# A fused linear-attention and bilinear-FFN kernel: dummy products to the column, g_norm out of the first place, a split load, wide weight loads and idle PSUM banks for block 1

## The chip, the cores and the metric

The kernel runs on one core of one Trainium2 chip. The metric is the device time in microseconds (us). A profile of one execution gives the span, which is some 1.7 to 2.0 us shorter than the time of the same execution; spans are compared with spans here and times with times. The granted clock is the share of TensorE's full clock that the profile records as given to it; 1.0 is full speed.

TensorE is the matmul engine, DVE the vector engine, ACT the scalar engine. POOL issues loads on a software queue; SP and ACT issue on hardware queues.

## The reference, cut to what matters

```python
# q, k, v: (8, 8, 576, 64)   w_a, w_b: (512, 1536)   w_out: (1536, 512)   fp32 in and out
kv  = np.einsum('bhsd,bhse->bhde', k, v)
out = np.einsum('bhsd,bhde->bhse', q, kv)
out = out / np.sqrt(np.mean(out * out, axis=-1, keepdims=True) + 1e-06) * g_norm
x   = out.transpose(0, 2, 1, 3).reshape(4608, 512)
return ((x @ w_a) * (x @ w_b)) @ w_out
```

## The kernel before

The kernel plans its own order. Each piece of work is a node with an engine, an estimated length, a priority and dependences with estimated latencies. A list scheduler then fixes the order of instructions on every engine. The real waits are semaphores, so a wrong estimate never gives a wrong result; it gives an order in which an engine stands still. PSUM banks, SBUF tiles and stores are rings that a node "takes" and "frees".

```python
    def order(self):            # cut
        ...
        t = max(self.ready(n), f)
        key = (f if t < f + 0.06 else t, n.prio)    # startable now: lowest prio; else earliest start
        if eng not in best or key < best[eng][0]:
            best[eng] = (key, t, n, way)
```

Batch 0 must be transposed, multiplied and normed before the FFN can start. TensorE has gaps in this stretch, and the kernel fills them with products of zeros whose result nobody reads.

```python
    def dummies(n):
        ps = banks[4]
        for _ in range(n):
            nc.tensor.matmul(ps[:], lhsT=zt[:, 0:128], rhs=zt, start=True, stop=True)
    ...
    dummies(10)
    nc.tensor.transpose(banks[5][:, 0:1], g_row, one)
    nc.vector.tensor_copy(g_col, banks[5][:, 0:1])
    ... # the plan is made here
    order, t = plan.order(), 5.7
    for n in order:
        if n.eng == "PE" and n.start < 22.0:
            dummies(int((n.start - t - 0.05) / 0.216))
            t = n.end
        n.emit()
```

Block 0 (512 tokens) uses plain products. Blocks 1 to 8 use a scheme of seven products per 2x2 block product, in six columns j. Per column there are products p1 to p7 into bank rings X, Y and Z, copies by ACT (ev), additions by DVE (comb), and at the end one multiplication of the a-half by the b-half on DVE. The last column's multiplication of block 8 is the last operand that the sums of the final output unit need.

```python
            X = Buf(RQ if bi == nb and j % 3 == 2 else RX)
            Y, Z = Buf(RY), Buf(RY)
            ... # cut
            p1 = pe(0.0, X, w_at(0, fs), lambda: b11, True, xdeps(lo, t0, t0 + n), [X])
            e1 = ev(0.0, u1, X, p1)
            ... # cut: p2, p6, p5, p7, p4, p3 with their copies and additions
            m = plan.add("DVE", fast_us(4 * n), pr + 0.6, mul, outs + [tk], (), [bb])
```

The loads of batches 2 to 7 (k and v directly, q through a transposing DMA) are planned with guessed latencies.

```python
        issue_us, q_us, ld["kv_us"] = (16.0, 5.5, 13.0) if dep is None else (9.0, 1.5, 11.5)
```

## Time and profile before

| What | Before | Where it is read |
|---|---|---|
| time, first three executions | 300.69 us (300.38 to 301.75) | times |
| span of the profiled execution | 298.7 us | first line of the page |
| TensorE busy | 290.9 us, 97% | part 1 of the page |
| block 0's first product | 16.27 us | timeline of TensorE |
| time that TensorE loses from 16 us to its last matmul | 3.58 us | start-to-start distances, below |
| last matmul's start to the end of the span | 4.0 us | timeline of TensorE |

Two of the first lines of the page of the kernel before; part 1 gives busy time, share of the span and number of instructions per engine.

```profile
span 298.7 us, 6687 instructions
PE 290.9 (97%) x2624; PEld 237.7 (80%) x2624; DVE 234.1 (78%) x433; ACT 192.5 (64%) x403; POOL 78.7 (26%) x97
```

TensorE binds the span as a whole. How much can still be won is not said by "97%", because the ends of matmuls are modelled. The view of waits of TensorE from 16 us on shows who held it; the columns are the waiting line, what released it, us in total, how often, and the longest.

```profile
PE bk L346 <- DMA qT<-scr: 1.0, 1, 1.0
PE bk L334 <- DMA abt<-in_q_dram: 0.2, 1, 0.2
PE bk L742 <- DVE T L711: 0.2, 1, 0.2
PE bk L846 <- DMA wo_t<-in_moe_w_out_dram: 0.2, 1, 0.2
```

The reader sees four waits: batch 3's transposed q, batch 1's q, block 1's operand T, and w_out. I also took the distance from one matmul's start to the next in the trace, less what the shape needs back to back (columns/2400 + 0.0025 us, which the 512-column products at 0.216 us and the 256-column ones at 0.109 us obey in this trace). It counts what the waits view drops below its threshold:

```
start   lost us   waits for
16.15   0.18      batch 0, squares by ACT
20.91   0.41      batch 1's q
44.67   0.14      block 1
45.48   0.37      block 1 (T)
47.95   0.26      block 1
65.68   0.34      w_out
80.89   1.15      batch 3's q^T
from 16 us to the last matmul: 3.58 in all
```

The lines shown are the losses of 0.14 us and more. Some 1.1 us of the sum are changes between 512-column products and groups of small ones, which take 0.09 to 0.10 us each.

The start of the kernel before: the timeline of TensorE and then of DVE. The columns are start, us, engine, line, operation, output<-input, shape and count; in brackets stand the idle time before it and who ended it.

```profile
6.21 0.19 PE L398 MATMUL bk<-one,g_row 1*128 1x1 f32 x1 [0.56 <-DMA g_row<-in_g_norm_dram]
7.11 0.56 PE L334 MATMUL bk<-ident,so 96*64 96x96 bf16 x12 [0.39 <-DVE so L494]
...
6.43 0.16 DVE L399 COPY g_col<-bk 128x1 f32<-128x1 f32 x1 [2.94 <-PE bk L398]
6.51 0.55 DVE L494 CAST so<-so 96x768 bf16<-96x768 f32 x1
```

A load of g_norm (two parts of 256 bytes) holds everything here. The transpose of g_norm stands first on TensorE and waits until 6.21; DVE copies it at 6.43; only then does DVE cast q, which had landed at 5.33, and only at 7.11 do the real transposes start.

The end of the kernel before, as the chain of waits has it from 285 us on (start, us, what):

```profile
284.93 0.22 PE bk L742 x2
285.15 9.84 PE bk L911 x90
294.99 0.03 issue
295.01 0.42 DVE o_sb L949
```

After block 8's last products (L742) stand 90 products of the final output unit (L911) without a gap, then one addition and a store. The last rows of TensorE's timeline show which products these are:

```profile
291.10 1.47 PE L911 MATMUL bk<-so,as 128*128 128x256 f16 x12
292.41 1.47 PE L911 MATMUL bk<-wo_t,as 128*128 128x256 f16 x12
293.72 1.25 PE L911 MATMUL bk<-so,abt 128*128 128x256 f16 x10
```

### The profile page before, as it was taken

The numbers are of one execution on the slowest core, as the hardware profiler recorded it, in microseconds if no ns is written. First come the engines' busy times: TensorE is split into PE (matmuls) and PEld (weight loads), VectorE is DVE, ScalarE is ACT, GpSimd is POOL, SyncE is SP. The second block draws the span as 40 slices with busy tenths as digits, with TensorE's granted clock in tenths as the row PEclk, the third lists the DMA queues.
The fourth block names the chain that finished last, engine by engine and source line by source line (L and its number), as shares of the span: only waits on it lengthen the run. The fifth ranks groups of instructions, "written<-read, shape, count | busy, mean of one in ns | idle before, by whom it ended". The sixth has DMA issues, their size and how long they took to land.

```text
span 298.7 us, 6687 instructions
## 1 busy us (share of the span) xinstructions
PE 290.9 (97%) x2624; PEld 237.7 (80%) x2624; DVE 234.1 (78%) x433; ACT 192.5 (64%) x403; POOL 78.7 (26%) x97
## 2 busy tenths in 40 slices
PE   7999999999899999999999999999999999999995
PEld 2545558855688898889888998889888888888884
DVE  4354979795878979698869986999599957897862
ACT  3757666866478667875688548954797556664521
POOL 8955830940191470190470000000000000000000
PEclk9999999999999999999999999999999999999999
DMA  8999999799999699699999400030004000300053
GB/s 178 191 200 199 195 160 157 98 167 167 235 101 164 76 201 189 56 103 165 208 142 161 143 2 0 2 143 1 2 0 143 1 2 10 133 1 2 2 170 112
DMA packets 99235, 32.72 MB, mean 110 GB/s; under 512 B 76676, under 2 KB 95108, under 8 KB 99204
## 3 DMA queue, kind: packets, MB, share of 16 engines
q0 software_dynamic: 78608, 18.44, 65.9%
q1 hardware_dynamic: 20096, 13.31, 20.4%
q10 hardware_dynamic: 500, 0.56, 0.6%
q8 instruction: 20, 0.33, 0.4%
q14 instruction: 11, 0.09, 0.1%
HBM read 37.75 MB, written 12.98 MB: 170 GB/s over the span
## 4 chain that ended last, share of the span: by engine, by line
PE 72%; DMA 21%; POOL 5%; issue 1%; DVE 0%; SPq 0%; POOLq 0%
PE bk L742 42%; PE bk L911 25%; DMA scr<-in_q_dram 8%; DMA qT<-scr 7%; DMA wb_t<-in_moe_w_b_dram 4%; DMA wa_t<-in_moe_w_a_dram 2%; PE bk L346 2%; PE bk L360 2%; PE bk L533 1%; POOL as L238 1%; POOL scr L566 1%; POOL so L238 1%; POOL wo_t L609 1%; POOL wa_t L295 1%; POOL wb_t L296 0%
## 5 line engine op out<-in xcount | busy, mean ns | idle before, releaser
L761 DVE TENSOR_TENSOR c<-bk,u 128x512 f16<-128x512 f32 x144 | 97.0, 687 | 27.2 <-ACT u L415 14.0
L415 ACT COPY u<-bk 128x512 f32<-128x512 f32 x144 | 82.3, 591 | 41.1 <-PE bk L742 38.5
L742 PE MATMUL bk<-xp,wa_t 128*128 128x256 f16 x288 | 55.0, 273 | 0.1
L742 PE MATMUL bk<-xp,wb_t 128*128 128x256 f16 x288 | 55.0, 273 | 0.0
L742 PEld LDWEIGHTS <-wa_t 128*128 128x128 f16 x384 | 37.4, 98 | 6.3 <-issue 0.3
L911 PEld LDWEIGHTS <-abt 128*128 128x128 f16 x384 | 37.5, 98 | 4.7
L369 DVE SCALAR_TENSOR_TENSOR xp<-bk,g_col,rs 128x288 f16<-128x288 f32 x64 | 32.6, 513 | 10.9 <-ACT rs L364 10.8
L742 PEld LDWEIGHTS <-wb_t 128*128 128x128 f16 x384 | 37.5, 98 | 4.4
L415 ACT CAST c<-bk 128x512 f16<-128x512 f32 x48 | 28.2, 590 | 17.6 <-PE bk L742 16.9
L911 PE MATMUL bk<-wo_t,abt 128*128 128x256 f16 x288 | 37.1, 273 | 0.0
L742 PE MATMUL bk<-T,sa 128*128 128x256 f16 x192 | 36.7, 273 | 0.2 <-DVE T L711 0.2
L742 PE MATMUL bk<-T,sb 128*128 128x256 f16 x192 | 36.7, 273 | 0.0
L364 ACT ACTIVATE rs<-bk,eps_t 128x288 f32<-128x288 f32 x64 | 32.2, 508 | 5.9 <-PE bk L360 5.4
L796 DVE TENSOR_TENSOR abt<-c 128x1024 f16<-128x1024 f16 x48 | 32.9, 688 | 1.8
L742 PEld LDWEIGHTS <-sa 128*128 128x128 f16 x288 | 28.0, 98 | 4.5 <-DVE T L711 0.5
L911 PEld LDWEIGHTS <-as 128*128 128x128 f16 x288 | 28.1, 98 | 3.5
L742 PEld LDWEIGHTS <-sb 128*128 128x128 f16 x288 | 28.1, 98 | 3.3
L356 ACT ACTIVATE sq<-bk 128x288 bf16<-128x288 f32 x64 | 25.2, 414 | 1.9 <-PE bk L346 1.7
L911 PE MATMUL bk<-so,as 128*128 128x256 f16 x192 | 25.7, 273 | 0.0
L943 ACT COPY o_sb<-bk 128x512 f32<-128x512 f32 x31 | 18.2, 587 | 11.1 <-PE bk L911 10.3
L572 POOL DMA_DIRECT2D k_t<-in_k_dram x24 | 21.2, 898 | 1.1 <-DMA wb_t<-in_moe_w_b_dram 0.5
L566 POOL DMA_DIRECT2D scr<-in_q_dram x12 | 19.6, 1635 | 1.9 <-issue 1.4
(100 smaller groups left out, 393.6 us busy)
## 6 DMA issues: line engine op xcount, KB each, us to landing
out_dram<-o_sb SPq DMA_DIRECT2D x20, 256.0 KB, 2.3
scr<-in_q_dram POOLq DMA_DIRECT2D x12, 288.0 KB, 8.0
k_t<-in_k_dram POOLq DMA_DIRECT2D x24, 128.0 KB, 8.2
v_t<-in_v_dram POOLq DMA_DIRECT2D x6, 512.0 KB, 10.1
out_dram<-o_sb SPq DMA_DIRECT2D x18, 128.0 KB, 2.3
wo_t<-in_moe_w_out_dram POOLq DMA_DIRECT2D x2, 768.0 KB, 9.4
wa_t<-in_moe_w_a_dram POOLq DMA_DIRECT2D x5, 256.0 KB, 10.8
wb_t<-in_moe_w_b_dram POOLq DMA_DIRECT2D x5, 256.0 KB, 10.8
```

The costliest lines, as they stand in the source:

```text
L238: nc.gpsimd.dma_start(out=t[n][:, hs, :, :], in_=src[b, hs].rearrange("h (sp c) d -> sp h c d", c=EC),)
L356: nc.scalar.activation(sq, self.x_ps[p, h][:, 0:HF], AF.Square)
L364: nc.scalar.activation(rs, self.s_ps[p, h][:, 0:HF], AF.Abs_reciprocal_sqrt, bias=eps_t)
L369: nc.vector.scalar_tensor_tensor(out=xcols(p, self.b * S + h * HF, HF), in0=self.x_ps[p, h][:, 0:HF], scalar=g_col, in1=self.rs[p, h], op0 ...
L415: ("ACT", act_us(n), lambda: nc.scalar.copy(*args())),
L566: nc.gpsimd.dma_start(out=scr[:, :, hl, :].rearrange("p s d -> s p d"), in_=qv[hl])
L572: nc.gpsimd.dma_start(out=kt[:, c], in_=ks[:, :, c, :])
L742: nc.tensor.matmul(ps.tile[:, i * n : (i + 1) * n], lhsT=lhs(w, sm)[:, kc, :], rhs=rhs()[:, kc, :], start=start and i == 0 and kc == 0, st ...
L761: lambda: nc.vector.tensor_add(cs(fi, h), full(ps), u.tile),
L796: nc.vector.tensor_mul(t, c[:, :, :, 0], c[:, :, :, 1])
L911: nc.tensor.matmul(ps.tile[:, sub * EH : (sub + 1) * EH], lhsT=lhs(slice(j, j + 1))[:, 0, sub * 128 : (sub + 1) * 128], rhs=rhs[:, j, :], ...
L943: lambda: nc.scalar.copy(o(fi, h), bank(X, every)), [dep], takes, frees,
```

## The change

The intent is to take away the waits named above: let the cast of q go ahead of g_norm, bring v of pair 0 on two hardware queues, load all weights in pieces of 256 columns, give block 1 banks that stand idle then, correct the guessed latencies so that other products are planned ahead of late data, and fill every gap of batch 0 to the column (at least 48) instead of in whole 512-column dummies.

```diff
-    WB = [(0, 128), (128, 256)]
-    WB += [(f, f + 256) for f in (768, 256, 1024, 512, 1280)]
+    WB = [(f, f + 256) for f in (0, 768, 256, 1024, 512, 1280)]
 ... (planned landing times W_AT and EARLY_AT adapted)
-        eng.dma_start(out=t, in_=src[0, 0:2].rearrange("h (sp c) d -> sp h c d", c=EC))
+        parts = ((0, 2, eng),) if n != "v" else ((0, 1, nc.scalar), (1, 2, nc.sync))
+        for h0, h1, e in parts:
+            e.dma_start(out=t[:, h0:h1], in_=src[0, h0:h1].rearrange("h (sp c) d -> sp h c d", c=EC))
-    def dummies(n):
-        ps = banks[4]
-        for _ in range(n):
-            nc.tensor.matmul(ps[:], lhsT=zt[:, 0:128], rhs=zt, start=True, stop=True)
+    def dummies(cols):
+        while cols >= 48:
+            n = min(cols, 512)
+            nc.tensor.matmul(banks[4][:, 0:n], lhsT=zt[:, 0:128], rhs=zt[:, 0:n], start=True, stop=True)
+            cols -= n
-    dummies(10)
-    nc.tensor.transpose(banks[5][:, 0:1], g_row, one)
-    nc.vector.tensor_copy(g_col, banks[5][:, 0:1])
+    dummies(10 * 512)
+    ... (both now nodes of the plan, not before 6.4 us; the copies of q^T of batch 0 all on DVE)
-        issue_us, q_us, ld["kv_us"] = (16.0, 5.5, 13.0) if dep is None else (9.0, 1.5, 11.5)
+        issue_us, q_us, ld["kv_us"] = (15.4, 4.3, 13.0) if dep is None else (9.0, 5.0 if b == 3 else 1.8, 13.0)
 ... (latencies: q 7.5 -> 8.0; w_out 5.0 -> 5.8 and 9.0 -> 10.6)
-            X = Buf(RQ if bi == nb and j % 3 == 2 else RX)
-            Y, Z = Buf(RY), Buf(RY)
+            X = Buf(RQ if (bi == nb and j % 3 == 2) or (bi == 1 and j % 3 == 1) else RX)
+            Y, Z = Buf(RY), Buf(RO if bi == 1 and j % 2 else RY)
-    wsum = weight_sums(42.0, reads)
+    wsum = weight_sums(44.0, reads)
-            dummies(int((n.start - t - 0.05) / 0.216))
+            dummies(int((n.start - t - 0.03) * 2370))
```

More of the change, by code (lines that the diff above doesn't have):

```diff
@@ L163 @@
     EPS = 1e-6
-    WB = [(0, 128), (128, 256)]
-    WB += [(f, f + 256) for f in (768, 256, 1024, 512, 1280)]
+    WB = [(f, f + 256) for f in (0, 768, 256, 1024, 512, 1280)]
     W_AT = {
-        "a": dict(zip(range(FC), (13.8, 15.3, 24.7, 24.7, 34.4, 34.4, 17.7, 17.7, 27.4, 27.4, 37.1, 37.1))),
-        "b": dict(zip(range(FC), (14.6, 16.2, 26.0, 26.0, 35.8, 35.8, 19.2, 19.2, 28.9, 28.9, 38.5, 38.5))),
+        "a": dict(zip(range(FC), (13.7, 13.7, 24.2, 24.2, 34.1, 34.1, 17.0, 17.0, 26.8, 26.8, 36.8, 36.8))),
+        "b": dict(zip(range(FC), (15.0, 15.0, 25.5, 25.5, 35.4, 35.4, 18.4, 18.4, 28.2, 28.2, 38.1, 38.1))),
     }
     EARLY_AT = [
-        [(5.2, 5.0, 6.5), (6.8, 8.0, 8.7), (9.4, 10.1, 10.8), (11.6, 12.3, 13.1)],
-        [(20.4, 21.9, 23.4)] * 2 + [(30.2, 31.7, 33.1)] * 2,
+        [(5.2, 5.0, 5.9), (6.5, 7.2, 7.9), (8.6, 9.4, 10.1), (10.8, 11.6, 12.3)],
+        [(19.8, 21.3, 22.8)] * 2 + [(29.8, 31.2, 32.7)] * 2,
     ]
@@ L296 @@
         nc.gpsimd.dma_start(out=wb_t[:, :, sl], in_=wb_v[:, :, sl])
-        if i in (2, 4):
-            early_load(early[1], 1, slice((i // 2 - 1) * HP, i // 2 * HP))
-    def dummies(n):
-        ps = banks[4]
-        for _ in range(n):
-            nc.tensor.matmul(ps[:], lhsT=zt[:, 0:128], rhs=zt, start=True, stop=True)
+        if i in (1, 3):
+            early_load(early[1], 1, slice(i // 2 * HP, (i // 2 + 1) * HP))
+    def dummies(cols):
[3 more added lines that the diff above has]
+            cols -= n
     def xcols(p, t0, n):
@@ L473, in slices @@
                 "DVE", dve_us(HF) + 0.06, pr,
-                lambda p=p, h=h: at.xt_op(p, h), [n4] + war, (), [x, rs],
+                lambda p=p, h=h: at.xt_op(p, h), [n4] + war + ([g_n] if at.b == 0 else []), (), [x, rs],
             )
@@ L499, in early_batch @@
             )
-            cp, eng, us = (nc.scalar.copy, "ACT", 0.56) if p % 2 else (nc.vector.tensor_copy, "DVE", 0.38)
+            cp, eng, us = (nc.scalar.copy, "ACT", 0.56) if p % 2 and b else (nc.vector.tensor_copy, "DVE", 0.38)
             n2 = plan.add(
@@ L553, in late_batch @@
         m = plan.add("ACT", 0.75, w0, kv_out, [n], (), [s])
-        slices(at, (w0 + 0.12 * (w1 - w0), w1), lambda p: [m, (load["qn"], 7.5)])
+        slices(at, (w0 + 0.12 * (w1 - w0), w1), lambda p: [m, (load["qn"], 8.0)])
     def load_node(b, prio, dep):
@@ L590, in transpose @@
             )
-        issue_us, q_us, ld["kv_us"] = (16.0, 5.5, 13.0) if dep is None else (9.0, 1.5, 11.5)
+        issue_us, q_us, ld["kv_us"] = (15.4, 4.3, 13.0) if dep is None else (9.0, 5.0 if b == 3 else 1.8, 13.0)
         ld["n"] = plan.add(
-            "POOL", issue_us, prio, issue, [(dep["qn"], 7.5)] if dep else [], [ld["k"], ld["v"]]
+            "POOL", issue_us, prio, issue, [(dep["qn"], 8.0)] if dep else [], [ld["k"], ld["v"]]
         )
@@ L609, in issue @@
                 nc.gpsimd.dma_start(out=wo_t[:, sl, :], in_=wo_v[:, sl, :])
-        return plan.add("POOL", 1.8, 50.0, issue, [(dep["qn"], 7.5)])
+        return plan.add("POOL", 1.8, 50.0, issue, [(dep["qn"], 8.0)])
     def std_block(win):
@@ L688, in out_sums @@
             ((t3, b22, b12, sub), (b12, b12, b11, sub), (t2, b22, b12, sub), (t4, b21, t2, sub)),
-            [(wo_n, 9.0)],
+            [(wo_n, 10.6)],
             list(o_reads),
@@ L855, in o_std @@
                     "PE", mm_us(OP, d_model), pr + 0.01 * f0, mm,
-                    [(wo_n, 5.0 if f0 + OP <= FC // 2 else 9.0), n1] + [muls[fc] for fc in range(f0, f0 + OP)],
+                    [(wo_n, 5.8 if f0 + OP <= FC // 2 else 10.6), n1] + [muls[fc] for fc in range(f0, f0 + OP)],
                     [ps] if f0 == 0 else [], [ab],
@@ L996, in o_unit @@
             return
-        p1 = prod(0, X, a11, b11, True, [(wo_n, 9.0)], [X])
+        p1 = prod(0, X, a11, b11, True, [(wo_n, 10.6)], [X])
         e1 = ev(0, 0, 0, p1, [ob])
@@ L1029 @@
         loads[b] = load_node(b, at_win[b - 1][0], loads[b - 1])
+    gb = Buf(RQ)
+    g_in = plan.add(
+        "PE", 0.07, 8.5, lambda: nc.tensor.transpose(gb.tile[:, 0:1], g_row, one), [plan.at(6.4)], [gb]
+    )
+    g_n = plan.add(
+        "DVE", 0.08, 8.5, lambda: nc.vector.tensor_copy(g_col, gb.tile[:, 0:1]), [g_in], (), [gb]
+    )
     early_batch(0, (4.0, 16.0))
```

## The prediction

> **What bounds the kernel.** TensorE: the page gives it 290.9 of 298.7 us busy. In its timeline I compared start-to-start distances of matmuls with what each shape needs back to back (512 columns 0.216 us, 256 columns 0.109 us). From block 0's first product (16.27 us) to the last matmul (294.70 us) only 3.0 us are lost: 0.4 at 20.9 (batch 1's first transpose waits for q, landed 20.86), 0.8 at 44.7 to 48.0 (block 1's start: the wait named is the DVE's T; the DVE is busy 5.00 of 5.00 us at 45 to 50), 0.3 at 65.7 (half of w_out lands at 65.64), 1.15 at 80.9 (batch 3's q^T lands at 80.85), the rest crumbs. Behind the last matmul's start stand 4.0 us, untouched. The change can win at most 3 us there plus what it takes off the 16.27 us before.
>
> **What moves.**
> - *Start.* Batch 0's transposes start at 7.11: before casting q (landed 5.33) the DVE stands at the g_norm copy (6.43), which waits for g_norm's DMA. The copy goes behind, so the transposes can start near 6.1. v of pair 0 (landed 6.38, behind k on one queue) may come 0.3 us earlier; the Trainium skill ("DMA: Bandwidth & Descriptors", Issuing engines are not separate DMA queues) says that a second queue brings no bandwidth, and I count on none. Pairs 1 to 3 come by the software queue in sequence, v of pair 3 at 12.72, which I expect unchanged. Its kv products started at 13.47, behind two dummies; now 12.8. From there to block 0 took 2.8 us, so block 0 starts near 15.6: **-0.7 us**. Weights are no limit: the first wa lands near 14.1, wb near 15.4.
> - *Wide loads.* Two 128-column pieces take 0.73 us each on the queue, one of 256 takes 1.34: about 0.25 us saved; later loads come 0.3 to 0.5 us earlier. Batch 1's q then lands about when TensorE reaches it: **-0.3 us**.
> - *Block 1.* More banks, T before the second half of the weight sums: **-0.4 us**.
> - *Later latencies for w_out and batch 3.* Other products go first: **-0.2** and **-0.8 us**.
> - *Dummies.* The clock has nothing to gain: the first ten take 0.43 us each, all after 6.3 us run at 0.216. (The skill, "TensorE: Matmul & The Clock Gate", Part 1, has the clock follow activity; the trace agrees.) Filling to the column gains **0**, and delays what comes earlier than planned, by under 0.2 us.
> - *New misfits* of the reordered schedule: **+0.4 us**.
>
> Sum -2.0 us: span 296.7, time **298.7 us**, 80% range 297.6 to 300.0. Faster by over 2%: 0.01; within 2%: 0.98; slower by over 2%: 0.01.
>
> **Right or wrong by:** block 0's first product at 15.3 to 15.9 us; pair 0's transposes at 6.0 to 6.4; v of pair 3 landing within 0.2 us of 12.72; last weight landing 38.3 to 38.7 (before 38.90); TensorE's waits at 20.9, 65.7 and 80.9 under 0.3 us each; lost time after block 0's start under 1.5 us; dummies still at 0.216 us; the tail unchanged.
>
> **What would make it wrong.** g_norm now lands behind half of v and stalls TensorE in front of pair 1; dummies planned to the column push batch 0's chain back; DVE overload in block 1 eats the gain; batch 3's q^T comes later, as a store now stands before it on the sync queue, and the 1.15 us wait stays or grows (then about 299.5).

## The result, and the profile after

The changed kernel took 299.82 us (median of six runs, 299.44 to 300.46). Six runs of the kernel before, the first three among them, gave 301.78 (300.38 to 301.96). Ratios are the mean time of one kernel's runs over that of the other's of the same rounds, so not quite the ratio of the quoted medians; here the ratio is 0.9948 with a 95% interval of 0.9924 to 0.9971. The change wins half a per cent, which counts as "same" at 2%. Against the 300.69 us known when the prediction was made the median fell by 0.87 us, and the two profiled spans (298.66 and 297.75) differ by 0.91 us. I had predicted 2.0. The paired means differ by about 1.6 us, and the medians of these six and six runs by 1.96, close to the 2.0; the profiles below show that this is no confirmation, since two terms of the sum failed. The kernel before scatters over 1.6 us and its profile fell on one of its quick executions, so the profiles may show less than the average gain; the traces can only explain the 0.91 us between these two executions.

The page of the kernel after, the same two lines as before.

```profile
span 297.8 us, 6705 instructions
PE 290.5 (98%) x2635; PEld 238.9 (80%) x2635; DVE 234.0 (79%) x435; ACT 192.4 (65%) x401; POOL 76.7 (26%) x95
```

TensorE's start and DVE's start after, from the timelines:

```profile
6.24 0.64 PE L336 MATMUL bk<-ident,so 96*64 96x96 bf16 x12
6.81 0.21 PE L1032 MATMUL bk<-one,g_row 1*128 1x1 f32 x1
...
5.42 0.77 DVE L494 CAST so<-so 96x768 bf16<-96x768 f32 x1 [1.93 <-DMA so<-in_q_dram]
7.29 0.15 DVE L1035 COPY g_col<-bk 128x1 f32<-128x1 f32 x1
```

The start works as intended. DVE casts q at 5.42 instead of 6.51, the transposes start at 6.24 instead of 7.11, and g_norm passes behind them without a wait. Block 0's first product starts at 15.55 instead of 16.27.

The waits of TensorE after, from 16 us on:

```profile
PE bk L533 <- DMA v_t<-in_v_dram: 1.2, 1, 1.2
```

Three of the four waits are gone in this profile (the one for w_out came back in two later ones with the same latency, 0.27 us in u3 and 0.86 us in w1). The wait near 80 us is not: TensorE now stands at batch 3's kv products (L533) for v, where it stood for q^T. By start-to-start distance:

```
start   lost us   waits for
16.45   0.29      second weight piece (w_b), landed 16.41
79.15   1.35      batch 3's v, landed 79.11
from 16 us to the last matmul: 2.12 in all
```

Block 1 shows it most plainly. TensorE's timelines at 44.9 us, before and then after:

```profile
44.89 0.38 PE L742 MATMUL bk<-xp,wb_t 128*128 128x256 f16 x2
45.48 0.39 PE L742 MATMUL bk<-T,sa 128*128 128x256 f16 x2 [0.21 <-DVE T L711]
```

```profile
45.33 0.38 PE L742 MATMUL bk<-xp,wb_t 128*128 128x256 f16 x2
45.55 0.38 PE L742 MATMUL bk<-T,sa 128*128 128x256 f16 x2
```

Two products of 256 columns need 0.22 us. Before, the next one started 0.59 us later; after, 0.22 us later.

The last matmul starts at 292.79 instead of 294.70, which is 1.91 us earlier, as predicted. The span is only 0.91 us shorter. The end of the chain of waits after shows the rest:

```profile
284.92 6.84 PE bk L911 x62
291.76 0.02 issue
291.79 0.59 ACT o_sb L943
292.38 0.02 issue
292.40 1.02 DVE o_sb L949 x2
293.43 0.33 DVEq L1088
293.76 0.60 DVE o_sb L949
```

The last rows of TensorE's timeline after:

```profile
290.28 1.47 PE L911 MATMUL bk<-so,as 128*128 128x256 f16 x12
291.59 1.47 PE L911 MATMUL bk<-wo_t,as 128*128 128x256 f16 x12
```

Before, TensorE ran to the end and one addition of 0.42 us followed. Now the chain leaves TensorE at 291.76 and ends in an ACT copy and a row of DVE additions. From the last matmul's start to the end of the span it is 4.96 us instead of 3.96.

### The profile page after: what moved, and what is told of

Read it like the earlier page. It is cut to its first block, busy times and chain, and to the rows that moved or that the text cites. A ratio compares the mean times of both kernels' runs of the same rounds, so it can differ in the third digit from the quotient of the medians.

```text
span 297.8 us, 6705 instructions
## 1 busy us (share of the span) xinstructions
PE 290.5 (98%) x2635; PEld 238.9 (80%) x2635; DVE 234.0 (79%) x435; ACT 192.4 (65%) x401; POOL 76.7 (26%) x95
## 4 chain that ended last, share of the span: by engine, by line
PE 71%; DMA 22%; POOL 4%; issue 1%; DVE 1%; ACT 0%; DVEq 0%; SPq 0%; POOLq 0%
PE bk L742 42%; PE bk L911 24%; DMA scr<-in_q_dram 8%; DMA v_t<-in_v_dram 4%; DMA wb_t<-in_moe_w_b_dram 4%; DMA qT<-scr 3%; DMA wa_t<-in_moe_w_a_dram 3%; PE bk L362 2%; PE bk L348 2%; PE bk L533 2%; POOL as L237 1%; POOL so L237 1%; POOL scr L566 1%; DVE o_sb L949 1%; POOL wo_t L609 1%
## 5 line engine op out<-in xcount | busy, mean ns | idle before, releaser
L415 ACT CAST c<-bk 128x512 f16<-128x512 f32 x48 | 28.1, 590 | 17.7 <-PE bk L742 16.9
```

The lines of the kernel that those rows point to most:

```text
L415: ("ACT", act_us(n), lambda: nc.scalar.copy(*args())),
```

## The experiments

Theories. The first (A) says that the tail is a matter of the planned order: the final output unit can't go faster than a chain that hangs on block 8's last multiplication, and the changed plan delays that one by putting products of the final unit ahead of it. Its rival is that the tail is noise or a slower store. The second (C) says that the wait near 80 us has only moved from q^T to v, and a later planned latency for v would remove it. The third (G) says that what is won at the start is partly swallowed by such a wait for a load, because the load does not come earlier when TensorE does. Rivals for the other parts are stated with their runs. Four groups of runs each shared one chip and its own runs of the kernel before: t1 to t3 with u1, u2 to u5, v1 to v4, and w1 alone.

Results, in us; the ratio is to the kernel before. All outputs are right.

| Run | Median (range) | Ratio (95%) | Profiled span |
|---|---|---|---|
| change | 299.82 (299.44 to 300.46) | 0.9948 (0.9924 to 0.9971) | 297.8 |
| t1 p1 early | 298.21 (298.13 to 298.76) | 0.9916 (0.9892 to 0.9939) | 296.4 |
| t2 p1 late, in the kernel before | 300.73 (299.84 to 302.44) | 1.0001 (0.9958 to 1.0044) | 299.8 |
| t3 = t1 + later v of batch 3 | 297.44 (297.26 to 297.73) | 0.9886 (0.9867 to 0.9904) | 296.0 |
| u1 whole dummies | 299.57 (299.37 to 299.95) | 0.9957 (0.9937 to 0.9977) | 297.6 |
| u2 g_norm first | 300.58 (299.10 to 300.64) | 0.9973 (0.9939 to 1.0007) | 298.6 |
| u3 narrow first pieces | 299.74 (299.33 to 300.12) | 0.9957 (0.9929 to 0.9984) | 298.3 |
| u4 v on one queue | 299.94 (299.54 to 300.33) | 0.9968 (0.9935 to 1.0) | 297.7 |
| u5 = t1 without block 1's banks | 301.13 (300.74 to 301.45) | 1.0003 (0.9976 to 1.0029) | 299.1 |
| v1 = t3 + g_norm first | 299.56 (298.95 to 301.16) | 0.9956 (0.9905 to 1.0007) | 299.4 |
| v2 = t3 + narrow first pieces | 297.40 (296.91 to 297.43) | 0.9887 (0.9846 to 0.9928) | 295.6 |
| v3 = t3 without gap dummies | 299.82 (299.03 to 300.65) | 0.9972 (0.9922 to 1.0021) | 298.8 |
| v4 = t1 with the old load latencies | 298.73 (298.59 to 298.85) | 0.9935 (0.9894 to 0.9976) | 296.9 |
| w1 = t3 + whole dummies | 297.70 (297.11 to 298.33) | 0.9879 (0.9855 to 0.9903) | 296.1 |

### t1: the last column's first product early again

```diff
-            p1 = pe(0.0, X, ...
+            p1 = pe(-14.0 if bi == nb and j == NJ - 1 else 0.0, X, ...
```

In the kernel before, the first product of block 8's last column had been planned early, into an idle bank. In the changed plan it stands behind the column before. The edit of the changed kernel only lowers its priority number, so that the planner takes it early.

> The changed kernel, but the first product of block 8's last column is given a priority that puts it in an idle bank early, as it stood in the kernel before; the order then leaves 90 products of the final output unit behind block 8's last product (as before), not 80. Theory A (the 1.0 us longer tail comes from ten final-unit products placed in front of block 8's last column, so that a dependency chain and not TensorE ends the kernel): block 8's last product starts about 1 us earlier than in the changed kernel (near 283.0 instead of 283.99), the last multiplication of block 8 too, the time from the last matmul's start to the end falls from 4.96 to about 4.0, span 297.75 to near 297.1, time 0.2 to 0.3% under the changed kernel. Theory B (the tail is set by the stores' queues or their landing): span unchanged within 0.2 us.

The end of the chain of waits of t1:

```profile
284.93 7.87 PE bk L911 x72
292.80 0.03 issue
292.83 0.42 DVE o_sb L949
```

TensorE ends the chain again, with one addition behind it. The span fell by 1.3 us to 296.43, although the last matmul moved by only 0.27 us (292.79 to 292.52). The times agree: u1, which ran beside t1 on the same chip and is the changed kernel but for its dummies, took 299.57 us (299.37 to 299.95), t1 298.21 (298.13 to 298.76). That the planned order makes the tail is shown. The sizes are best seen in one table; all values are from the traces, "behind" counts the products of the final unit that stand behind block 8's last product.

| Kernel | block 8's last product starts | behind | its last multiplication ends | last matmul starts | last addition ends | span |
|---|---|---|---|---|---|---|
| before | 284.88 | 90 | 286.68 | 294.70 | 295.44 | 298.66 |
| change | 283.99 | 80 | 285.95 | 292.79 | 294.36 | 297.75 |
| t1 | 282.69 | 90 | 284.49 | 292.52 | 293.25 | 296.43 |
| t2 | 286.15 | 78 | 287.95 | 294.78 | 296.35 | 299.78 |

With 90 products behind, the last addition ends 0.73 to 0.74 us after the last matmul's start; with 78 or 80, 1.57 us. The same holds in all 15 profiles: the distance from the last matmul to the span's end is 3.9 to 4.0 us with 90 behind and 4.9 to 5.0 us with 78 or 80. In contrast, the distance from the last multiplication's end to the span's end is 11.79 to 11.99 us in every one of them. So the end moves with that multiplication. The change brought it forward by 0.73 us, not by 1.91. From the last addition to the end of the span, the store, it is 3.2 to 3.4 us in all four kernels of the table, so a slower store makes at most 0.2 us of the difference.

The timelines show what lies between. The second group of 12 products `so,as` of the final unit starts at 290.28 after and at 291.10 before. The last ACT copy and the additions hang on it, and from its start to the end of the span it is 7.46 to 7.56 us in all 15 profiles. With 90 products behind, 22 others follow this group and cover the copy and the additions. With 78 or 80, only 12 follow: the ten products `so,abt` that end the kernel before were used earlier, in front of this group, where TensorE needed work.

The stronger half of theory A, that the unit can't go faster than the chain through the multiplication, is not shown. In the chain of waits above TensorE has no gap up to 291.76, and the first group of `so,as` in the changed kernel started 1.92 us after the multiplication's end, while the third of the four sums on DVE, the one it reads, was ready after 1.38 us. About half a us there is the plan's.

### t2: the same product late in the kernel before

```diff
+            late = p3s[-1:] if bi == nb and j == NJ - 1 else []
-            p1 = pe(0.0, X, w_at(0, fs), lambda: b11, True, xdeps(lo, t0, t0 + n), [X])
+            p1 = pe(0.0, X, w_at(0, fs), lambda: b11, True, xdeps(lo, t0, t0 + n) + late, [X])
             ... (p3 of each column is appended to p3s)
```

> The kernel before, with the same product made to wait for the column before it, so that it stands late as in the changed kernel: 78 products stay behind block 8's last product instead of 90. Theory A: last matmul's start roughly unchanged (294.7), block 8's last product about 1.3 us later, the tail grows from 3.96 to about 4.6 to 5.0, span +0.5 to +1.0 us over before. Theory B: span as before within 0.2 us.

The chain of t2 ends as that of the changed kernel does:

```profile
286.42 7.34 PE bk L913 x66
293.76 0.02 issue
293.78 0.59 ACT o_sb L945
294.38 0.02 issue
294.40 1.02 DVE o_sb L951 x2
295.42 0.33 DVEq L1083
295.75 0.60 DVE o_sb L951
```

The last matmul stands where it stood in the kernel before (294.78 against 294.70), but the span is 1.12 us longer: the tail of 5.0 us can be made in the old kernel by the order alone. The times don't resolve it (ratio 1.0001, with runs from 299.84 to 302.44), so the confirmation rests on the profile. This profile also had g_norm land late (TensorE released at 6.91 instead of 6.21) and block 0 start at 16.97, 0.70 us later than in the profile of the kernel before; by the last multiplication of block 1 it was down to 0.04 us (t2 stood neither at batch 1's q nor at w_out, where the kernel before lost 0.41 and 0.34), and near 80.9 both stood at the same wait. That gave theory G.

### t3: v of batch 3 planned later

```diff
-... 5.0 if b == 3 else 1.8, 13.0)
+... 5.0 if b == 3 else 1.8, 16.0 if b == 3 else 13.0)
```

> As the first run, and the kv products of batch 3 planned 3 us later (latency 16.0 instead of 13.0). Theory C (the 1.35 us lost at 79.15 is only a wrong place in TensorE's order: v lands at 79.11 and other products could go first): the loss there falls to 0.3 to 0.6 us, the last matmul starts 0.7 to 1.0 us earlier than in the first run, span near 296.3. Theory D (batch 3's loads are a bound: nothing else is ready): as much time is lost around 79 to 82 under another name, span as the first run within 0.2 us.

The waits of TensorE in t3 from 16 us on:

```profile
PE bk L382 <- DMA wb_t<-in_moe_w_b_dram: 0.6, 1, 0.6
```

The wait of 1.2 us near 79 us has gone from the list; by start-to-start distance 0.26 us remain at 81.38. In this run the second weight piece landed late (16.88 us) and cost 0.78 us at block 0, and still the span fell by 0.48 us against t1. Theory C stands in its second half: planning v later removes the wait (what made v late is taken up below). At a ratio of 0.9886 this version beats both kernels.

### u1 and w1: whole dummies instead of the column

```diff
-            dummies(int((n.start - t - 0.03) * 2370))
+            dummies(int((n.start - t - 0.05) / 0.216))      # and the old dummies(n)
```

> The changed kernel with the dummy rule of before (whole 512-column dummies only, gaps under 0.27 us left empty); nothing else moves. My theory (the clock has nothing to gain): matmuls from 6 us on still at 0.216 us for 512 columns, block 0's first product 15.3 to 15.6 (15.55 in the changed kernel), span within 0.25 us of the changed kernel. Rival (the fill to the column keeps the clock up): some products of the first 16 us at 0.43 us, block 0 later by over 0.5 us.

> The third run's kernel (no wait for batch 3 left to swallow a late start) with whole 512-column dummies only, by the rule of before. If filling to the column is worth nothing beyond the whole dummies: all runs at a granted mean clock of 0.996 or more, block 0's first product 15.3 to 15.9, time within 0.4 us of the third run (297.44). If it is needed to hold the clock: some runs at 0.994 or less, and those slower by 1 us or more.

u1 is the changed kernel with the old whole dummies, w1 is t3 with them, so that no wait for batch 3 can swallow a difference. Neither is distinguishable from the version with dummies to the column: 0.9957 against 0.9948, and 0.9879 against 0.9886, with intervals 0.004 to 0.005 wide. (w1's profile was not free of waits either: it lost 0.86 us at w_out, at 61.38.) The mean granted clock in the runs of u1 was 0.997 to 0.999. Filling to the column brought nothing that these runs can resolve, as predicted.

### v3: no dummies in the gaps

```diff
-            dummies(int((n.start - t - 0.03) * 2370))
+            pass
```

> The third run's kernel without any dummy products in batch 0's gaps (the first ten or so before it stay). If the dummies hold the clock up: a half-speed window of 3.4 us between 6 and 16 us, granted mean clock near 0.994, block 0's first product later than 15.54 by 0.5 us or more, time up by 0.3 to 1 us. If they are for nothing: clock as before (0.998 to 1.0), block 0's first product 15.0 to 15.6, time within 0.3 us.

The view of windows, of v3 and then of t3; the first column is the window in us, and PEclk is the third value from the end.

```profile
5.00:10.00 5.00, 3.06 (x61) 2.32 (x61) 2.14 (x5) 2.04 (x7) 4.89 (x8) 0.78 1.29 200
10.00:15.00 5.00, 4.68 (x54) 2.79 (x51) 2.38 (x6) 3.49 (x11) 4.25 (x7) 0.50 1.39 198
15.00:20.00 5.00, 4.54 (x14) 1.57 (x13) 2.49 (x5) 3.26 (x9) 2.13 (x4) 0.50 1.37 198
```

```profile
5.00:10.00 5.00, 3.84 (x72) 2.86 (x72) 2.48 (x6) 2.38 (x8) 5.00 (x8) 1.00 1.30 200
10.00:15.00 5.00, 4.95 (x59) 3.01 (x59) 2.91 (x7) 4.61 (x15) 4.22 (x7) 1.00 1.41 200
15.00:20.00 5.00, 4.38 (x25) 1.95 (x24) 2.12 (x4) 2.80 (x7) 2.12 (x4) 1.00 1.37 197
```

Without dummies the granted clock falls to half from 7.78 to 21.44 us; block 0's products then take twice their 0.216 us, block 0 starts at 17.16 instead of 15.54, and from block 1 on every multiplication on DVE is 2.87 us later. The median is 2.4 us over t3's, more than the 0.3 to 1 us expected, since the clock stayed low for 13.65 us and not for 3.4. So the dummies hold the clock. The old whole ones did it already, and that is why the finer ones gain nothing.

### u2 and v1: g_norm in the first place again

```diff
     dummies(10 * 512)
+    nc.tensor.transpose(banks[5][:, 0:1], g_row, one)
+    nc.vector.tensor_copy(g_col, banks[5][:, 0:1])
     ... (the two nodes of the plan emit nothing)
```

> The changed kernel with the g_norm transpose and copy put back in front of batch 0 on both engines, as in the kernel before; the schedule behind is the same. My theory (the start was won by taking g_norm's landing out of the way of pair 0's casts): pair 0's transposes start at 7.0 to 7.8 us instead of 6.24, block 0's first product at 16.0 to 16.9 instead of 15.55, span 0.3 to 1.0 us over the changed kernel, and its runs spread by about 1 us as those of before do, because g_norm's landing moves (6.2 in the trace of before, 6.9 in the second run's). Rival (the software queue's loads bound batch 0: v of pair 3 lands at 12.6 either way): block 0's first product within 0.2 us of 15.55.

> The third run's kernel (tail mended, batch 3's kv products late; span 295.95, time 297.44) with the g_norm transpose and copy in front again. Theory G (in the changed kernel a late start was nearly free, as the wait for batch 3's loads at 79 us swallowed it: 2.5 us later at block 0 became 0.84 us at block 2 on): here that wait is gone, so a start that is late by x us costs more than half of x: block 0 at 16.2 to 18.0 and time 0.5 to 2 us over the third run. Rival (the start is absorbed anyway, by weights and other loads): time within 0.3 us of the third run.

u2 undoes this part in the changed kernel, v1 in t3. The timeline of TensorE in v1 at the start:

```profile
4.72 0.38 PE L305 MATMUL bk<-c 128*128 128x512 bf16 x1
7.06 0.19 PE L400 MATMUL bk<-one,g_row 1*128 1x1 f32 x1 [1.96 <-DMA g_row<-in_g_norm_dram]
8.07 1.18 PE L336 MATMUL bk<-ident,so 96*64 96x96 bf16 x22 [0.41 <-DVE so L496]
```

TensorE stands 1.96 us for g_norm here (1.64 us in u2), and afterwards the clock was at half speed for a while (8.04 to 11.46 us in u2, 7.84 to 14.67 in v1). How much later things came than in the kernel without this edit, in us:

| | block 0's first product | DVE multiplications of block 1 | from block 2 to the last |
|---|---|---|---|
| u2 against the change | +2.50 | +2.19 | +0.84 |
| v1 against t3 | +4.22 | +3.42 | +3.42 |

In u2 the delay shrinks from 2.19 to 0.84 us in the stretch where the changed kernel waits 1.35 us for v; u2 has no wait left there. In t3 that wait is gone, and v1 passes its delay on in full. (0.78 us of the first figure of v1 are the late weight of t3's own run.) Block 0 came later than I had expected in both (18.05 against 16.0 to 16.9, 19.75 against 16.2 to 18.0); I had not expected the clock to fall. Theory G stands: while a load sets the pace at 80 us, what is won or lost before it counts only in part. The two edits also show that g_norm's position is worth the more, the later the load happens to land, and in the kernel before it landed early enough in the profiled run (6.21).

### u3 and v2: narrow first weight pieces

```diff
-    WB = [(f, f + 256) for f in (0, 768, 256, 1024, 512, 1280)]
+    WB = [(0, 128), (128, 256)]
+    WB += [(f, f + 256) for f in (768, 256, 1024, 512, 1280)]
```

> The changed kernel with the first 256 columns of both weights loaded as two pieces of 128 again; TensorE's order is the same. Theory E (wide loads win 0.25 us of queue time but cost as much at the start, as the first wb now lands whole): first wb lands near 14.2 to 15.7 instead of 16.41, the 0.29 us lost at 16.45 vanishes, all later weights land 0.2 to 0.5 us later (last 38.5 to 38.9 instead of 38.33), span within 0.3 us of the changed kernel. Rival (wide loads pay): span over 0.3 us longer.

> The third run's kernel with the first 256 weight columns in two pieces of 128. The third run lost 0.78 us at 16.9 waiting for the first wb of 256 columns (landed 16.88). Theory E: narrow pieces take that wait away, and later loads come 0.3 to 0.5 us later: 0.2 to 0.5 us lost at batch 1's q (20.7), time within 0.4 us of the third run either way. Rival (wide loads are worth their 0.25 us and more): over 0.4 us longer.

The narrow pieces bring the second one earlier and lose 0.30 us (u3, at 20.72) or 0.20 us (v2, at 20.79) to batch 1's q instead of 0.29 us (change) or 0.78 us (t3) at the second wide piece. The ratios don't differ: 0.9957 against 0.9948, and 0.9887 against 0.9886. The wide loads moved a small loss and are worth nothing that can be seen.

### u4: v of pair 0 on one queue

```diff
-        parts = ((0, 2, eng),) if n != "v" else ((0, 1, nc.scalar), (1, 2, nc.sync))
+        parts = ((0, 2, eng),)
```

> The changed kernel with v of pair 0 on the sync queue alone, as before. My theory (a second queue brings no bandwidth and v is not what the start waits for): v lands at 6.3 to 6.5 (6.36 for the later half now), block 0's first product within 0.15 us of 15.55, span within 0.25 us of the changed kernel. Rival (the split pays): first product over 0.3 us later.

In u4 v of pair 0 landed at 6.66 us; split, its halves landed at 6.00 and 6.36. Block 0 started at 15.81, which is 0.26 us later and more than I had expected, but the span is the same (297.73 against 297.75) and so is the time (0.9968). The Trainium skill ("DMA: Bandwidth & Descriptors", Issuing engines are not separate DMA queues) says that transfers of all issuing engines run on the same 16 engines, and that issuing on several saves only the time of issue. Here not even that was saved: v was issued at 1.20 us in u4, its halves at 1.20 and 1.21 us in the changed kernel. The 0.3 us at landing can't be put down to the split: in u4 the loads it leaves alone were later too (k of pair 0 by 0.13 us, q by 0.20, v of pair 3 by 0.32), and the kernel before, with v on one queue, had it at 6.38. Nothing of the difference reached the end; by block 1 u4 was 0.05 us ahead, as its second weight piece landed earlier (15.61 us).

### u5: block 1 without the idle banks

```diff
-            X = Buf(RQ if (bi == nb and j % 3 == 2) or (bi == 1 and j % 3 == 1) else RX)
-            Y, Z = Buf(RY), Buf(RO if bi == 1 and j % 2 else RY)
+            X = Buf(RQ if bi == nb and j % 3 == 2 else RX)
+            Y, Z = Buf(RY), Buf(RY)
```

> The first run's kernel (last column's first product early, so that the tail is the same) with block 1's idle banks taken away again. Compare with the first run (span 296.43). Theory F (the banks and the later weight sums together removed the 0.8 us lost at 44 to 48, and without the banks the loss comes back): 0.5 to 1.5 us lost between 43 and 52 us, last matmul and span 0.5 to 1.7 us later than in the first run. Rival (the order of T and the weight sums alone did it): under 0.2 us lost there, span within 0.3 us of the first run.

The window of block 1's start (the columns after the length are busy time of PE, PEld, DVE, ACT and POOL), of u5 and then of the changed kernel:

```profile
45.00:50.00 5.00, 4.35 (x36) 3.37 (x35) 5.00 (x11) 3.05 (x6) 0.00 (x0) 1.00 1.47 169
```

```profile
45.00:50.00 5.00, 5.00 (x48) 4.46 (x46) 5.00 (x11) 3.47 (x8) 0.00 (x0) 1.00 1.48 166
```

DVE is busy for all of the 5 us in both, but with the idle banks TensorE runs 48 matmuls in this window and without them 36. u5 lost 1.94 us in block 1, then 0.78 us at batch 3's v and 1.00 us at its q^T. The last matmul came 2.68 us later than in t1, and the span rose by 2.66 us, more than I expected; 0.33 us of it stood already at block 0's first product, which the banks don't touch. The banks are the part of the change that the runs show to be worth most in the stretch that it was meant for. It is more than the 0.77 us lost there before, because the changed plan without the banks is worse in this place than the old plan was. I did not run the moved priority of the weight sums (42 to 44) by itself, so how it and the banks share the gain stays open.

### v4: the old load latencies

```diff
-... (15.4, 4.3, 13.0) if dep is None else (9.0, 5.0 if b == 3 else 1.8, 13.0)
+... (15.4, 4.3, 13.0) if dep is None else (9.0, 1.5, 11.5)
```

> The first run's kernel (span 296.43; 1.41 us lost at 78.9 waiting for batch 3's v) with the planned latencies of batch 3's loads as in the kernel before (1.5 and 11.5 instead of 5.0 and 13.0). If the change's new latencies did what they were for, the loss around 77 to 82 grows from 1.4 to 2.2 us or more and span by 0.6 us or more; if they only moved the wait from q^T to v, the loss stays 1.2 to 1.6 us and span within 0.3 us of the first run.

v4 is t1 with the old latencies of batches 3 to 7. It loses 0.34 us at v (77.03), 0.90 us at q^T (79.68) and 0.24 us at 81.82, in all 1.48 us, where t1 loses 1.41 us at v alone. The span is 0.47 us longer, but so were the multiplications of block 1 already (block 0 started at 16.06 us instead of 15.53), before any of these loads is used. So the traces show no gain by the new latencies: they moved the wait from q^T to v. What removed it is the later latency of v in t3 (16.0 for batch 3).

## Why the prediction was right or wrong

The sum, term by term. The middle column is read from the two profiles.

| Term of the prediction | Predicted | Between the profiles |
|---|---|---|
| start, to block 0's first product | -0.7 | -0.72 |
| batch 1's q (wide loads) | -0.3 | -0.41 |
| block 1 | -0.4 | -0.77 |
| w_out | -0.2 | -0.34 |
| wait near 80 us | -0.8 | +0.20 |
| new misfits (here: second weight piece) | +0.4 | +0.29 |
| crumbs | 0 | -0.17 |
| last matmul's start | -2.0 | -1.91 |
| behind the last matmul's start | 0 | +1.00 |
| span | -2.0 | -0.91 |

**The start was right.** The transposes were predicted at 6.0 to 6.4 and came at 6.24; block 0 was predicted at 15.6 and came at 15.55; v of pair 3 landed at 12.62 (predicted 12.72, unchanged); the last weight landed at 38.33 (38.3 to 38.7). The reason was right too: the cast of q no longer stands behind g_norm. The loss after block 0's start was predicted under 1.5 us; by the formula above it fell from 3.40 to 2.15.

**The step that failed most is "Behind the last matmul's start stand 4.0 us, untouched."** They became 4.96. I had treated the tail as a constant added to TensorE's end. It is a second chain beside TensorE's work: the last products that are copied by ACT, the copy, DVE additions, store. In the kernel before, 22 products stood behind the group that this chain starts from and covered it, so the tail looked like a constant. The planner was given other times and put ten more products of the final unit ahead of block 8's last product. That brought the last multiplication forward by 0.73 us only; other products of the final unit then had to fill in early, and 12 were left behind that group. The span came forward by 0.91. t1 (order mended, span -1.3) and t2 (order spoiled in the old kernel, span +1.1) show this; a look at the planned order around block 8 before the run could have shown it.

**"Later latencies ... batch 3 -0.8" failed.** The wait grew from 1.15 to 1.35 us. I had looked at q^T alone because the profile named it alone. (The prediction names a wait that stays, with about 299.5 us, as a risk, but with another cause: q^T later behind a store. It came 0.77 us earlier.) Before, the second half of v landed at 78.03 and q^T at 80.85. In the changed kernel that half of v was issued 1.26 us earlier (66.89 against 68.15) and landed 1.08 us later (79.11), 2.43 us behind the first half instead of 1.22; q^T landed at 80.08 and no longer held anything up. In the profile of u1, which has the same plan, that half of v landed at 77.87, and TensorE lost 1.07 us at q^T instead (80.51). So the changed plan comes too early for both loads, and which one it stands at differs between executions. t3 removes the wait; v4 shows no gain by the new latencies.

No run was made to find why the half took longer, but the kept traces narrow it down. In the changed kernel a packet of 16 KB of the queue that carries instructions (q8), 1.07 us long, started at 76.73, just when this half was next to land; in the kernel before such a packet came at 78.54, after the half. In the five profiles in which such a packet was served, at least in part, between the two landings (change, t1, t3, u4, v2) the second half landed 2.20 to 2.77 us behind the first, in the other ten 0.79 to 1.30 us; in u3, where it came before the first half had landed, the first half was the late one (5.11 us behind the load before it, elsewhere 3.14 to 4.29). The two go together in all 15; that the packet is the cause was not tested by moving it.

**The terms were added as if independent, and they are not.** While a load sets the pace near 80 us, a gain at the start is in part returned there: u2 shows 2.2 us of delay shrinking to 0.84, v1 shows 3.42 us passed on whole once the wait is gone. That the last matmul came out at -1.91 against -2.0 is therefore partly luck: the wait near 80 us missed by 1.0 us, and the terms that won more than predicted (block 1 by 0.37, w_out by 0.14, batch 1's q by 0.11, new misfits by 0.11, crumbs by 0.17) nearly cancelled it.

**"The first wb near 15.4" was wrong by one microsecond.** It landed at 16.41 in the changed kernel and cost 0.29 us, which lies within the +0.4 us that I had set aside. Against narrow pieces the cost is a draw (u3, v2).

**"The clock has nothing to gain" was right for the filling to the column, and read from too little.** I read it from one profile. Among the 32 runs of the kernel before that were timed beside the experiments, 14 had a mean granted clock of 0.989 to 0.994, as a short stretch at half speed gives; all six of the changed kernel had at least 0.996. The slower clock did not make those runs slower (mean 301.10 against 301.19 us), which fits a delay at the start that later waits for loads swallow, but that was not tested by itself. v3 shows what the dummies are for: without them the clock falls, and 2.9 us of span or 2.4 us of the median time are lost.

**What stays open.** The paired means say 1.6 us and the profiles 0.9. Why the kernel before scatters (299.2 to 302.2 in those 32 runs) was not settled; its clock doesn't explain it. Nor was it tested why some loads of the software queue land late, beyond the coincidence with packets of the instruction queue.

## What to carry to other kernels

Before adding up waits that a change removes, follow the last chain back past the busiest engine: the end may hang on something else, here on how many products were left to cover an ACT copy and the additions behind it, and a planner that reorders work can move the busy engine's end without moving that. A wait for a load is a reset: gains ahead of it count only as far as the load comes earlier as well, and if one of two loads of a batch is blamed, look at when the other one lands, and at more than one execution. When a plan is driven by estimates, change one estimate at a time and look at the order of the last stage first.

## What the Trainium skill lacked or had wrong

- "Perfetto Trace Analysis", Optimization Strategy, tells the reader to take the engine in question, find the gaps between its slices and determine what blocks them. That found the waits, but it misses the tail: TensorE had no gap there, and the span still ended with another chain. In 15 profiles the span ended 11.79 to 11.99 us after block 8's last multiplication, and 3.9 to 5.0 us after the start of TensorE's last matmul.
- "TensorE: Matmul & The Clock Gate", Part 1, lets the clock fall after an idle window of about 3.4 us, and its rule is to have no idle gaps longer than that. Here it fell with far shorter gaps: after a single wait of 1.96 us in v1, and in v3 where the longest idle stretch in the 3.41 us ahead of the fall was 0.82 us. What was low is the busy share: TensorE was busy for 0.37 (v1), 0.43 (u2) and 0.62 (v3) of the 3.41 us ahead of the fall. v2 had as long an idle stretch (0.83 us) in its first 3.41 us at full speed, was busy for 0.65 of them and kept its clock, as t2 did at 0.65. The same Part does report that frequent short idle stretches made the clock swing in another kernel, but gives no share. Agreeing with the page: the stretches at half speed last 3.41 us or a multiple (3.41 in u2, 6.83 in v1, 13.65 in v3), and 512 columns take 0.43 us in them.
- "DMA: Bandwidth & Descriptors", Anatomy of one DMA, gives about 2 us as the fixed cost of a load on the software queue, and no figure for a small load on a hardware queue beside large ones. Here the two small loads of g_norm, issued by 2.0 us in the kernel before (2.5 us in u2 and v1), released TensorE only at 6.21 us, beside the loads of q, k and v, and at 6.85 to 7.06 us in t2, u2 and v1. No run here measures an idle queue.
- No page says that loads can be late while instructions are fetched. In a row of loads 256 columns of weights mostly took 1.30 to 1.37 us each on the software queue and 128 columns 0.70 to 0.76 us, but in the traces of both kernels one piece near 16 us took 2.4 to 2.5 us (15.65 to 18.09 before, 13.95 to 16.41 after), at the time when a packet of the queue that carries instructions was served (15.57 and 14.30). The second half of batch 3's v shows the same in all 15 profiles, as told above. It isn't so for every load: in u4 and v4 such a packet was served at 14.37 and 14.93, and the weight piece that was next took 1.31 and 1.34 us. The cause was not tested.
